# Turning the softmax weights of three batches by a transposing DMA instead of TensorE, in an attention and Fourier-filter kernel with a searched instruction order

## The chip, the core and the metric

The kernel runs on one core of a Trainium2 chip. A core has five engines that run side by side and wait for each other through semaphores: TensorE (PE: matrix products and transposes, with PEld for its weight loads), VectorE (DVE), ScalarE (ACT), GpSimd (POOL) and SyncE (SP, which here only issues DMAs). The metric is the time of one execution on the device, in microseconds; the median of three runs of the kernel before is 189.91 us (189.7 to 190.37).

## What is computed

For each of 8 batches and 8 heads, 32 packed queries attend to 576 keys; then 576 queries attend to the 32 packed results, used both as keys and values. The result, 576 x 512 in a batch, is projected to three parts, the second part is convolved with a filter along the sequence (by Fourier transforms), the three parts are multiplied, and the product is projected once more.

```python
def sm_attn(qq, kk, vv):
    s = scale * np.matmul(qq, kk.transpose(0, 1, 3, 2))
    a = np.exp(s - np.max(s, axis=-1, keepdims=True))
    return np.matmul(a / (np.sum(a, axis=-1, keepdims=True) + 1e-09), vv)
p_packed = sm_attn(p, k, v)              # 32 rows a head
x = sm_attn(q, p_packed, p_packed)       # 576 rows a head; heads are then joined to 512 columns
x1, x2, x3 = split(x @ w_proj)
x2_conv = np.fft.irfft(np.fft.rfft(x2, n=S, axis=1) * H, n=S, axis=1)
return (x1 * x2_conv * x3) @ w_out       # 8 x 576 x 512, float32
```

## The kernel before

The 32 packed rows of each head make it cheap to keep the second attention in factors: the softmax weights `a2` of one batch are 576 rows (sequence) x 256 columns (head, packed row), and the packed values times `w_proj` are `qm`, 256 x 1536. The three parts `x1`, `x2`, `x3` are products of the two. Each batch passes four stages, and four batches are in work at a time, one in each stage:

- `front`: first attention, scores of the second attention, exponentials, and the normalised weights `a2` (GpSimd writes them for all batches but the first);
- `turn`: `qm`; the Fourier transform of the weights (`fp`, `fpt`, then `fa`); and the **turned weights** `a2t`, with the 256 columns on partitions, in two halves `t`;
- `middle`: the spectrum times the filter (`f`, then `gm`), and the gate `w = x1 * x3` from products of `qm` with `a2t`;
- `back`: the inverse transform (`x2`) times the gate gives `y`, and the output projection `o` is stored.

The weights lie in one buffer of 128 partitions x 1152 columns: four row tiles of 256 columns each, and a fifth, joined tile of 128 columns for the last 64 rows. The turning before is done by TensorE into PSUM and copied by VectorE:

```python
# turn(b)
for t in range(2):
    tp = pst(f"a2tp_b{b}", [P, S], FP16)
    nc.tensor.transpose(tp[:, ds(COL0[4] - 64 * t, P)], a2c, ident)
    for i in range(4):
        to = tp[:, ds(COL0[i], P)] if i != 2 else ...     # [cut] tile 2 goes into two pieces of 64
        nc.tensor.transpose(to, a2n[:, i, ts(t, P)], ident)
    nc.vector.tensor_copy(out=a2t[:, t, :], in_=tp[:])
```

```python
# middle(b): four gates of 512 columns (one a part m), and one of 64 columns for all parts
x1, x3 = psm(...), psm(...)
for x, c0 in ((x1, 0), (x3, 2 * DM)):
    for m in ms:
        for t in range(2):
            nc.tensor.matmul(x[:, m - ms[0], :], qm[:, t, ds(c0 + m * P, P)], a2t[:, t, cols],
                             start=(t == 0), stop=(t == 1))
nc.scalar.copy(out=x1s[:], in_=x1[:])
nc.vector.tensor_tensor(out=w[...], in0=x1s[:], in1=x3[:], op=ALU.mult)
```

The queries of batches 4 to 7 and the keys of batches 6 and 7 are turned by transposing DMAs already (`TURNED`, `KEYS`), issued from SyncE. The last product of the kernel is the fifth row tile of batch 7. Its two column halves go through two PSUM tiles; ScalarE copies one and VectorE the other, and two DMAs of 64 rows x 512 columns store it, one from SyncE and one from ScalarE:

```python
for u in range(2):
    rows = out[b - 1 + u, 0:512, :].rearrange("(p i) c -> p i c", i=4)
    (nc.sync, second)[u].dma_start(rows[64:128, 3, :], os_[64 * u:64 * u + 64, :])
```

No operation is issued in the order in which this code stands. A recorder takes all operations down and issues them in an order of its own: a string of priorities (`PRIORITY`, one number for each operation), which a search found, is played against a model of the engines' times inside the kernel file. All engines' instructions therefore carry the same source line (L538), and rows of the profile are told apart by the names of tiles. At the start TensorE is kept busy by products that nothing uses (`spin`).

Of the kernel before, what the change touches and what calls it, by code (L numbers as in the profile page):

```python
# [14 lines left out]
FP16 = mybir.dt.float16  # L15
# [4 lines left out]
P = 128  # L20
# [23 lines left out]
def _constants(S):  # L44
# [42 lines left out]
    'c-oy-2|QHm`#)ziBV@}q$-b}ILqe1#S<_+(QCblyS-Q3q6)7nx*OIa&WG5L#Qp%bw`;vWM;+D?&kC{0$!@d8{?{|OiG0r*f`<(aLzR&l0g<vs='  # L87
    '-skz=M^>B>C98^O79=;F+~z2#*^_&Aw(_gw@3h6d`$6M;p%eO@bfY=Fi=#RWN-2G@iNBm%a|9kab)~&68y;M>&-z&J>u@98+tu6WNM5tTp1|z#'
    'qN=p|rB#7u465h(xW9?n6X6(xO9%Y5o!Y~Vd5uTyvI9)Kk{_km+>Y2kq&E`(wW?P9sFRkdd!Sr^NE}AYes9%X?nBnbHmZ_nD-Bnas&><q?Gdd@'
    'agRzO9Fs4eI)1LutKQ+6yGz~G@Al~}em{~bQltED8=tkdw>WMUq+8?k^4OId=CA0)CUW!yJMK1h$A^2>XrHn<=si!HtR58dY7^%lTfApvBP(j}'  # L90
    'XK1H#MvGZi2Wh<=RN*mR3Ti#4ZRBGnWvrmze8J~}flqdhj1?a@tLLPO-KJTUX{YU%gA*f#YdP}n^tMYCwvDSg>leK~BH%1@WQaM_M%9T=PUB?X'
    'ZNCl=5AztGcz<EZH~dD8o>?L)TmO8V=kd$l)U2K-cHqeS4zwuGiM{S%C~vW(*VE9)(9JM5h3cXi-|Ml8<t)%=&!Q&>r6rE$u|9?z?(KcA{=p~2'
    'WY1y1W@QGqS;LH%|A&_L@z9f27oDSnnVpXDT~s#H_ElnbK5OM;d_j%<x*Ux?!yaX<l%j~Xw~?UKG`lX1oVp>~sxnV%xfQ#R=d%9MR9i00`{vFF'
    'lpvS1%pvy|ZPIRs9tYU%E!=j4u@Y;8jj!GJu-D}JPFv1=FRlrbmRaA218rDgjc`9%u+l2~1WPLK$-}SA1w4=V3tmv86_XyGw_n=6IwG#lHl)uc'
    'HO;MFtrvo808<2A_z&q%Vqe}^Rw@r>URiBD9C5CdcUW~-{554`eJ_*#DD!Wjz0m?~P{|CtUsvI-r(*UdahGo&4e2_;&BnBNStAatUoCUDoaE3?'
    'YDO<-)ckh*8vlDx;+)sPKm2ACs>QxzSOSHXxii&(FNRY!$)I%sdM*oVj`m265bg3{%S!G!@6~T$F&A6!`nvC3t1{1=k{?s2q7jFq>c0K9tzSFp'
    'a;AMHx?Kzfop-tJwDdLdm*6?6z$L^jZ+1d=hnb)0aeXzc-Whj)b_ruMN!`<W7p#wK$;nr0sVi}SUh!|EP7K;^MPHRQ)DFTLS=_xDqNv6(+cMsp'
    '08}ybEYk|{*$Bxn6ktS8@6%c3?3&`brYGg#>=k-2Le6%}t<<Q74-RVKAJ00)+WILgSEhSq+J}0FCwWAL-8*&5x@!L0W5(mUhwlV4J`r)2ZVa!%'
    ';(A1~2Esn+XDKJkq8TDJm_&*muvzU~)Irr4<Vx2HCXJSX#h+suRHkbF<P3X1UO!Z(Q{G*Rdb(6m)1KF{qNNq3e@5T$_ioeQbK4GYI$3Z6Ug>1#'
    '%#Ij$Po1h;3ZyxLxhf$b#QyA7<;`7RO}&e6mseJQoG3D#%zeh8a(*wLoVv=2x-h?~+X+2-Md|HIEYb?9iu^pg#94LpC2V%esbZJ4nYH$a@`~)_'  # L100
    '4tw*`o9zf+#Oe5nkHbr%g+_73+vsc?<TMSO1NVI5f5OTr|4~)>y<Z2%F?7EDDyPIN!(YsaQOceM=&`d(Sdm|hBJ7fX<<QP;OMLFtv7lq_cyCEi'
    'R-)ohVGHe7{g*}TI&{bH4@Eodr=fRYm6(s8$eL_lO2;|&UhH-0I-VEsywW2}HT=}djDkl9t*th{i2QGPld6Ly^qjRu(_@b^uEl6BajQ!4H<as%'
    'E{MjqT1>cz38x64#<VTpK7E~#_eXl!8&!<YL}TKZY<CJawAH6f%$dPp(SkQ)I;ME;fJ<Q1)pT6Z$mJEObA8`3%jZvo_}_oqnp*tjTxMCv$|Hdg'
    'lS0o^F6k~ISTie~u3(v+d`zmn<z;gXEkECmRgZnCrb+5-eewO<yBEE6_3yHq^P5sfvOab7eEwP)*I6=FTer~mSMj}6QF#H)@f$x*`FeC1F4b=x'
    '>M(ED3jd?kp3YuNyx&qx!tTKS)fP_I=IwKD_KRAp+IZQR7#JzA#JMd_?o4NmMTJUfObbYHpJ1z2qZguuB6}HSIRy(w>hr#>pa#Y)ZC>Y>%eU+f'
    '9Gr>#)HiU;Oih+;cu(;sZ@X)W?;@U`PCs4{Q~j=6RBH5?13w!Zzp`OGZ+Z9Ng$mD7W1L5@Wq`YvSFnX+LF=qM!>=7Y+a|Bw;+O9hKJb#QVrS%R'
    'acUde*N7KIv1Xp{s`wv#iOlR3K!>PADHaU<tm|D^$R0o|&^|WGIGh}meKl8;WzeZP>R{O2=Ald7I@aY41%ti8QggLU35?ssN8)^~3!Z?`ZadaX'
    'X`d4PT3%c`jnm3%sX+5=UKJ`k>t?Le!oM(ab5U40kA>aCh5ulua5c_7@wQuRwEMl={+Ay(2Ho-Uwfo~j?7cUJcWtjbI%_&#*74cD$NzAc+wFU1'
    ';l{yN4NymD`_-77r$4W*4%s}4?B5rK^LKb(9crN+_;V^>^U7Jrm^v=ruM4w`heV=^)7k@sVghpG-&)KZ{B$rbIk^G8LPM{|I|7)y(eB?X<6h-#'
    'ZrZs;*Tz%c!qX#8mgVf{=(wYA<i9)Azm6BIj=p<K_<2HR8msu7i?lL&30~*gbn;VC=iGnH+VDM9YoM<<G$@&~t4#fAcy_?U8@K&e>1Usf>QDaE'  # L110
    'Qi*is!<cS6irsb0H_SZ#v4H7Jt;Oc>olEDxT{E<f-aWEoyvg<uss}wh^j4eRO-tE0=sOGjwYxV1!Xg4M#iupp&9_%_wQm~ChZ2~al48=oEj{d*'
    '4y?`U&dI<fgyKHr)r8>^s*?um3!BsDlY+X_@4mV9BsJ~X%gBz37hzB7jGbB-yzb&UKBmW|NQ5}szdzX>)RWy*FW6V}>GgtT;_8)WuQDzs%XDmi'
    ')&05j`ZDv(Hfc^x-ATjCZi1{^VsTe;Ubg*ta)^aXceCawn^Ov#Xq#Ko3!I+cxffgA^}^ymsAI)hCYYA`mZy7P756q^goa}y+yZZS1EK;l82Gh<'
    'Z|$$CG`WMS1{3#cidB7YWO^TE9uE`XY1`)%rg3q<$`zM@ikO@OU2b{V+;aW%!;4GIM+=L&gsYT3WBb_4?p(~ayr)s<d9@^PuF3%YxZK}GJmV<N'
    'w~X%afV8BQtomSurLC@oDLwZgldp6sbQQgqJxv*lR5f>vt{T;adFNg@!`wH_q}af`{V!%7GzV>{#jlh58M||72U*$C$|ZFbzgG&|8k<&{D$8+`'
    '#nr_FjkW#tDY&A+?)1j&k@5Vh{+jZ^sZTZ4RrO=N<;NA3V|KjoJ#l1e_c<JcH*S(;{`u+Pcpv|$Or3z+$rtVC-X@mD#CR|D50B5I{KhALeV=X9'
    '>-+I#q^Zwt{#Pf9NrCAOqs-VJu5X^Y#pHWrVB32ZAXkT^QpRjX2p8`ck@7g~No-1OaLaJZCDvQt#p$s-w(2c$-i2ce%S$@y25iJPVU=WVHGdvs'
    'US2urNShJeUz?Xwno)~;RGRtnQFLN;Q)vKu2@}RxoxU+xzbMip!#Gwa-0G!i#+S;>&n4xr^P@OYq_N=|yw(9(jePO<6K1g-Y+M2#@}sqqf~O+j'
    '(|=uFO*#+3Qo98?=<>><C&lP~bVq1_JY8RNJ}vg$E3Mh~F;+E+_qzH02fl_qyb8IF#uYg;35F}Dw_n@e*;Q)idWQYS=yxV<UM0&9T(QXm%3@m-'
    'RciH5UvhQ*smqxhHTw2!RaFK19aix;&bce|FC|1d->Y$5WC)-a=Qb?hPnGA8i9|hYzu)_4aiS|jpy{gbN@`k>U{PiXlcv%@nYelGSpLVy2bd>W'  # L120
    'Wps8hXM`l)EctdPKmWJ&yrizAPD|?3telW+AA4W@F1Cd0X=dJA1!<p4lz!w<y|OZ^waIb2gzN*Ay>$tVEy_avNBj0PWU~D_%k`%Fyt4-1F`L{x'
    '$*yswxm79Fy6TddvW2l1_m_pci>7cKDxxL&N*G2a9$a`>Uq7h)w7+Oc<Q+RN-*oS?n5@DCYAcO0!{$byZspqyN|+mtp(`0a79Y|ZUd@hLnr^RW'
    '{7h5&p3RqOv8`nZJ^AAcCZ7(2+3e8SIC`jWVi|w|7=;4xfA|68e;|kgQ7909BfQZ7AYmQ`2^ap3pMXiCYd69(2oPTZ@-8rG5Y}Osynx&Y3#7-j'
    'ZDB+Rkpch|@<7^{C;<P<LDWvQKUo7vRF3y}ZICn&rI1MwZv^q8d`c1}O09hZ0@UuoWC!pXA;bt$$kwJHV!#L!_>aN0T|k(q4u(;rcu|%K14T3+'
    'c?H*Y0jUP?Uk$Ql1pVZIfK*`xVNw|2HCxu)C71&unI`N3!5}fR01{ysL=nsf)*QsU4Xt?&0pu?L5J@{Z&SZE%q=ofKgEp8=3JCr`MAQL6L^b3c'
    'Ng@a|0W>A~00u*i2co9{8G^L5)WG`vF9*>A3<g6>9cx00kX%v)n{cPaP$sBAO~L~KZZO#wa*{ww(C}75gt2a47$ye_fJv%B(gX2Jh+L7B?8C$`'
    '!o;KkWLd;m5F{akIzbx{^&bF7KoL1ZFcJ_DVG*L?Bvg^1MqO7(nkiI42Irbrz#0HyB-_9$wEiNO2u#TY3A}{=5Jas4zXDNMib7=|Ou!rxC87XC'
    '9W$6jYg7Y8PAy^kO=t?00e>T^|4e2`Fp>J(geLj`!W4c*Ds%0H293sR#M}LwXgfeAB_y7R9W=z9NYq4@p;^<g(F_nqNErmEfI$Hsl0Z^`A+l1U'
    'G`NBC$=pMIt%E;`T0M%2RjHzge?n2U7QBTtG*n#&2L9y$i3I@?3yly>8l;X8d=kI|A+FHS5HymrNp2M|Qp1Q5C>lao@S6h&nQp|vTBlj-%Orq-'
    '8yNwn>WUld4hakdfdG+?DS-cn+NCH4VCY{CczvTI%mHM6#{WR1%J3RdD2U<&saQd3Y$II;M8T8@!w9PJCleH*<Vd;^>&XdPg9bp^4llnEyC{JA'  # L130
    'Sb%Ud@mgaE=%4BiqMS_#{STsAfv6HkPBe&^4Ezs+N-K=8_y5ZdAo%z4{6}FzoJl={dKQ0}AiDx>@R|~NsvNKLcVp+K*Z@+zq4d9X)~(|~gp4S-'
    'qLdZ5?#w`uCc~LfSQJPC8yOR(YK;K!Psd1L-Ek2hn+a{~Jft0=zZpYTgFul~8k7~n;f1h5=IFl}LUl~0q>{p=z`EuIuS*UU@c@*Q*?NxrKThot'
    '$p'
)

# [69 lines left out]
class Tick:  # L205
    n = -1
# [338 lines left out]
def kernel(  # L545
# [11 lines left out]
    nc = Recorder(tc)  # L557
    B, H, S, D = q.shape
# [593 lines left out]
```

## Time and profile before

| what | value |
|---|---|
| time, median of 3 | 189.91 us |
| span of the profiled execution | 187.6 us |
| TensorE | 175.1 us busy, 93% of the span, 2363 products |
| VectorE | 145.3 us busy, 77% |
| GpSimd | 138.0 us busy, 74% |
| ScalarE | 122.2 us busy, 65% |
| DMA | 31.96 MB in 49002 packets |

The page counts an engine as busy from the start of an instruction to its modelled end. TensorE's products are pipelined: the next starts long before the one ahead of it has ended, so the duration of one in the table of groups is its latency, and what a product costs in a dense stream is the distance from its start to the next start. A run of n equal products in the timeline lasts one latency and n - 1 such distances. In the chain of waits, followed back from the last instruction, each step is put down to what released it.

### The profile page before, as it was taken

How to read it: one execution, taken by the hardware profiler on the slowest of the kernel's cores; microseconds unless marked ns; L12 is line 12 of the kernel's file. 1: busy time of each engine (PE TensorE's matmuls, PEld its weight loads, DVE VectorE, ACT ScalarE, POOL GpSimd, SP SyncE). 2: the span in 40 equal slices, each digit the busy share in tenths (PEclk: the TensorE clock that was granted, in tenths of full speed). 3: DMA queues.
4: the chain of work that ended last, by engine and by line, in shares of the span. 5: the costliest groups of instructions: out<-in, count | busy, mean ns of one | idle time of the engine just before them, and what ended most of it. 6: DMA issues, size and time to landing. Idle time of an engine off the chain costs nothing.

```text
span 187.6 us, 5689 instructions
## 1 busy us (share of the span) xinstructions
PE 175.1 (93%) x2363; PEld 112.5 (60%) x2363; DVE 145.3 (77%) x274; ACT 122.2 (65%) x261; POOL 138.0 (74%) x111
## 2 busy tenths in 40 slices
PE   0999879999999999999999999999999999999990
PEld 0456546666756766865577557657655566555770
DVE  7368797967569789977789978977688898796560
ACT  2457757758989988667965496469659934434240
POOL 7533447795966899989949997799189979979300
PEclk9999999999999999999999999999999999999997
DMA  5999999999999999999999999958601500332374
GB/s 145 297 200 196 204 204 201 259 203 188 200 227 275 177 202 192 148 131 188 263 197 225 158 156 200 179 133 272 166 2 59 169 3 0 121 103 59 121 256 131
DMA packets 49002, 31.96 MB, mean 170 GB/s; under 512 B 21008, under 2 KB 43920, under 8 KB 48976
## 3 DMA queue, kind: packets, MB, share of 16 engines
q0 software_dynamic: 29456, 17.11, 64.4%
q1 hardware_dynamic: 18944, 13.70, 31.7%
q10 hardware_dynamic: 576, 0.79, 1.6%
q8 instruction: 18, 0.29, 0.7%
q14 instruction: 8, 0.07, 0.1%
HBM read 35.39 MB, written 9.44 MB: 239 GB/s over the span
## 4 chain that ended last, share of the span: by engine, by line
PE 82%; DVE 7%; POOL 4%; ACT 3%; issue 1%; POOLq 0%; DVEq 0%
PE x_b L538 29%; PE o_b L538 17%; PE f_b L538 9%; PE fp_b L538 5%; PE s_b L538 4%; PE hp L538 4%; PE pv_b L538 3%; PE kTp_b L538 3%; PE qp_b L538 2%; PE a2tp_b L538 2%; DVE zs L538 2%; PE spin L538 1%; DVE tt L538 1%; POOL tt L538 1%; POOL a2n L538 1%; PE qTp_b L538 1%
## 5 line engine op out<-in xcount | busy, mean ns | idle before, releaser
L538 PE MATMUL x_b<-a2t,qm 128*128 128x64 f16 (+1 forms) x256 | 46.1, 286 | 0.8 <-ACT qm L538 0.7
L538 DVE TENSOR_TENSOR tt<-f_b,h 128x1024 f32<-128x1024 f32 x32 | 38.6, 1219 | 5.6 <-PE f_b L538 5.2
L538 POOL TENSOR_TENSOR gm<-tt,tt 128x512 f16<-128x512 f32 (+1 forms) x30 | 39.6, 1346 | 0.9 <-DVE tt L538 0.3
L538 POOL TENSOR_TENSOR tt<-tt,tt 128x1024 f32<-128x1024 f32 x14 | 33.2, 2378 | 8.5 <-DVE tt L538 8.4
L538 PE MATMUL o_b<-wout,y 128*128 128x512 f16 (+1 forms) x144 | 38.2, 356 | 0.0
L538 PE MATMUL x_b<-ac,gm 128*128 128x64 f16 (+3 forms) x300 | 36.6, 249 | 0.0
L538 ACT COPY x1s<-x_b 128x512 f32<-128x512 f32 (+1 forms) x40 | 21.8, 545 | 16.4 <-PE x_b L538 10.8
L538 DVE TENSOR_TENSOR w<-x1s,x_b 128x512 f32<-128x512 f32 (+1 forms) x40 | 24.7, 628 | 7.1 <-ACT x1s L538 4.5
L538 PEld LDWEIGHTS <-gm 128*128 128x128 f16 x300 | 23.1, 98 | 10.0 <-issue 1.0
L538 ACT ACTIVATE os<-o_b 128x512 f32<-128x512 f32 (+1 forms) x36 | 20.0, 572 | 11.2 <-PE o_b L538 10.8
L538 ACT CAST qm<-qp_b 128x512 f16<-128x512 f32 x48 | 25.4, 605 | 2.6 <-PE qp_b L538 2.5
L538 ACT ACTIVATE e<-s_b 96x384 f16<-96x384 f32 (+1 forms) x48 | 23.5, 524 | 4.2 <-PE s_b L538 3.7
L538 PE MATMUL f_b<-qm,fa 128*128 128x512 f16 x80 | 25.3, 379 | 0.3 <-POOL fa L538 0.3
L538 DVE SCALAR_TENSOR_TENSOR y<-w,x_b 128x512 f16<-128x512 f32 x32 | 21.2, 682 | 5.3 <-PE x_b L538 5.0
L538 PEld LDWEIGHTS <-qm 128*128 128x128 f16 x256 | 17.9, 98 | 11.3 <-ACT qm L538 1.2
L538 PEld LDWEIGHTS <-a2n 128*128 128x128 f16 x240 | 16.6, 98 | 9.1 <-DVE a2n L538 1.6
L538 POOL TENSOR_TENSOR fa<-ez 128x512 f16<-128x512 f32 x15 | 19.0, 1275 | 2.7 <-ACT ez L538 2.6
L538 POOL TENSOR_TENSOR a2n<-e,zr 128x1152 f16<-128x1152 f16 x7 | 14.9, 2130 | 4.5 <-DVE zr L538 4.4
L538 PEld LDWEIGHTS <-y 128*128 128x128 f16 x144 | 13.0, 98 | 7.4 <-issue 0.8
L538 ACT COPY ez<-fp_b 128x512 f32<-128x512 f32 x16 | 9.3, 591 | 5.7 <-PE fp_b L538 4.6
L538 DVE TENSOR_REDUCE zs<-e 128x36 f32<-128x1152 f16 (+2 forms) x10 | 11.1, 1107 | 0.9 <-ACT e L538 0.8
L538 POOL DMA_DIRECT2D kn<-in_k_dram x8 | 6.5, 815 | 6.8 <-PE s_b L538 2.4
(82 smaller groups left out, 288.5 us busy)
## 6 DMA issues: line engine op xcount, KB each, us to landing
out_dram<-os SPq DMA_DIRECT2D x24, 256.0 KB, 2.4
kn<-in_k_dram POOLq DMA_DIRECT2D x8, 576.0 KB, 14.9
vn<-in_v_dram POOLq DMA_DIRECT2D x8, 576.0 KB, 11.1
qn<-in_q_dram POOLq DMA_DIRECT2D x8, 512.0 KB, 14.2
out_dram<-os SPq DMA_DIRECT2D x15, 128.0 KB, 3.2
wp<-in_moe_w_proj_dram POOLq DMA_DIRECT2D x3, 512.0 KB, 15.9
w<-in_moe_filter_fft_dram SPq DMA_DIRECT2D x2, 512.0 KB, 6.2
out_dram<-os SPq DMA_DIRECT2D x15, 64.0 KB, 2.1
```

Of the source, the lines that this page charges most:

```text
L538: ins = op.call(*op.args, **op.kw).ins
```

## The change

It has four parts.

- For batches 5, 6 and 7 (`FLIP`) the ten TensorE transposes and two VectorE copies of a batch go away. One transposing DMA from SyncE turns the whole buffer `a2`, 128 x 1152, into nine blocks of 128 x 128.
- The DMA leaves the columns in the order of the blocks, not in the order that the gate wants. So the products of the gate take their right operand in pieces for these batches: 512 columns become pieces of 256 (two blocks apart from each other), 64, 64 and 128 columns. For each piece the two halves `t` follow each other. The gate of the last 64 columns stays one product a half.
- The fifth row tile of batch 7 is stored by four DMAs of 64 rows x 256 columns instead of two of 64 x 512: two from each queue.
- The model's cost of the packets of a store is set from a rate of 22.7 to 18 bytes a ns, and the string of priorities is new, so that instructions on all engines stand in a new order.

The point of the first part is to take work off TensorE and VectorE and two PSUM tiles a batch; the last stores are cut so that one column half may leave before the other is ready.

```diff
+        s["a2t"] = sb([P, 9 * P], FP16, tag="a2t", name=f"a2t_b{b}")
+        if b in FLIP:
+            nc.sync.dma_start_transpose(s["a2t"].rearrange("p (x r) -> p x r", r=P), s["a2"][:])
 ...
-        for t in range(2):
+        for t in range(0 if b in FLIP else 2):
             tp = pst(f"a2tp_b{b}", [P, S], FP16)
 ...
+        def turned(t, cols):
+            if b not in FLIP:
+                return [(slice(0, cols.stop - cols.start), a2t[:, t, cols])]
+            if cols.start:
+                return [(slice(0, 64), a2b[:, 4 + t, 64:128])]
+            return [(slice(0, 256), a2b[:, 2 + t:7 + t:4, :]), (slice(256, 320), a2b[:, 8, ts(t, 64)]),
+                    (slice(320, 384), a2b[:, 4 + t, 0:64]), (slice(384, 512), a2b[:, t, :])]
 ...
-                    for t in range(2):
-                        nc.tensor.matmul(x[:, m - ms[0], :], qm[:, t, ds(c0 + m * P, P)], a2t[:, t, cols],
-                                         start=(t == 0), stop=(t == 1))
+                    for pieces in zip(turned(0, cols), turned(1, cols)):
+                        for t, (c, right) in enumerate(pieces):
+                            nc.tensor.matmul(x[:, m - ms[0], c], qm[:, t, ds(c0 + m * P, P)], right,
+                                             start=(t == 0), stop=(t == 1))
 ...
-                    (nc.sync, second)[u].dma_start(rows[64:128, 3, :], os_[64 * u:64 * u + 64, :])
+                    for c in range(split):
+                        c = ts(c, DM // split)
+                        (nc.sync, second)[u].dma_start(rows[64:128, 3, c], os_[64 * u:64 * u + 64, c])
 ...
         if self.reads and self.engine != "POOL" and piece > 1000:
-            self.piece_ns = piece / 22.7
+            self.piece_ns = piece / 18
 ...                                            # and a new string PRIORITY
```

## The prediction

> **What bounds the kernel now.** I read the page's busy times and its chain of waits first, then TensorE by stretches of time and the waits of TensorE alone.
>
> ```profile
> PE 175.1 (93%) x2363; PEld 112.5 (60%) x2363; DVE 145.3 (77%) x274; ACT 122.2 (65%) x261; POOL 138.0 (74%) x111
> PE 82%; DVE 7%; POOL 4%; ACT 3%; issue 1%; POOLq 0%; DVEq 0%
> 30.00:90.00 60.00, 59.50 (x983) 40.34 (x981) 48.10 (x93) 48.32 (x105) 51.03 (x41) 1.00 1.38 200
> 90.00:130.00 40.00, 40.00 (x572) 25.93 (x571) 34.84 (x60) 27.79 (x65) 34.43 (x25) 1.00 1.18 195
> PE spin L538 <- DVE ppk L538: 4.8, 1, 4.8
> PE x_b L538 <- ACT qm L538: 0.7, 1, 0.7
> PE a2tp_b L538 <- DVE a2n L538: 0.7, 2, 0.4
> ```
>
> The third and fourth lines are stretches of the trace: length, then TensorE's busy time (59.50 of 60 us, 40.00 of 40 us), weight loads, VectorE, ScalarE, GpSimd, granted clock 1.00. TensorE is the bound from about 30 us to the last product. Its waits (the last three lines: us in total, times, longest) are a start of 4.8 us and then less than 1 us each, all in the first 30 us or so. So work that TensorE is spared is nearly all gain, and work that VectorE or GpSimd is spared gains nothing by itself. After TensorE comes a tail:
>
> ```profile
> 182.64 0.38 ACT L538 ACTIVATE os<-o_b 128x256 f32<-128x256 f32 x1 [0.38 <-PE o_b L538]
> 183.05 0.53 ACTq L538 DMA_DIRECT2D out_dram<-os  x1
> out_dram<-os ACTq DMA_DIRECT2D x1, 128.0 KB, 3.3
> ```
>
> The last copy starts at 182.64 us, the last DMA is issued at 183.05, it takes 3.3 us to land (third line: size, then us from issue to landing), so 186.4; the remaining 1.2 us to 187.6 are the program's end.
>
> **What one product costs.** In the timeline of TensorE a run of n products lasts one latency and n - 1 distances from start to start:
>
> ```profile
> 147.39 0.51 PE L538 MATMUL x_b<-ac,gm 128*128 128x64 f16 x12
> 151.47 0.72 PE L538 MATMUL x_b<-ac,gm 128*128 128x288 f16 x5
> 153.97 0.33 PE L538 MATMUL a2tp_b<-wc,a2n 128*128 128x128 f16 x3
> 154.60 0.49 PE L538 MATMUL fp_b<-wc,a2n 128*128 128x256 f16 x3
> 148.39 1.27 PE L538 MATMUL x_b<-a2t,qm 128*128 128x512 f16 x12
> ```
>
> The first: latency 0.193 us (the groups' mean for 64 columns), so (0.51 - 0.193) / 11 = 29 ns for 64 columns, each with its own weights. The third: latency 0.220, (0.33 - 0.220) / 2 = 55 to 56 ns for 128 columns, which is what a transpose costs. The fourth: (0.49 - 0.272) / 2 = 109 ns for 256. The last row mixes 512 and 64; 512 alone, start to start, is 216 ns (153.10 to 153.97 us in the same timeline holds four). The weight loads, 98 ns each in the groups, hide behind products at every one of these sizes.
>
> **What the Trainium skill says.** Three places bear on this.
> - "TensorE: Matmul & The Clock Gate", section "Back-to-back issue gap", gives N/2.4 + 2.5 ns for an isolated warm product, so 29, 56, 109 and 216 ns: the trace agrees. The same section gives some 81 ns as sustained for a stream of weight loads and products of 128 columns; this trace shows 56 with weight loads in between, and I take 56.
> - "VectorE: DVE Perf Modes", section "The three transpose paths", puts a 128x128 transpose at 390 ns on TensorE and 1309 ns by DMA. In this trace TensorE pays 56 ns of its stream for one, and a whole transposing DMA of 128 x 576 lands after 2.6 us; both are far cheaper when many follow each other.
> - "DMA: Bandwidth & Descriptors", section "Issuing engines are not separate DMA queues": DMAs of all engines share the same 16 and interleave. The trace agrees: turning the keys took 8.0 to 12.7 us around 97 to 100 us while inputs were loading, and 2.6 once they were in.
>
> **The change, part by part.**
>
> (1) Transposes leave TensorE: 3 batches x 10 x 56 ns = **-1.68 us**.
>
> (2) The gate is cut in pieces. One product of 512 columns (216 ns) becomes four of 256, 64, 64 and 128: 109 + 29 + 29 + 56 = 223 ns, 7 ns more. There are 2 parts (x1, x3) x 4 gates x 2 halves x 3 batches = 48 of them: 144 more products, **+0.34 us**. Weights now change at every product of 64 columns, but so they do in the 29 ns run above. Net with (1): **-1.34 us**, 2363 products become 2477.
>
> (3) VectorE loses 6 copies of 0.454 us (the group of a2t copies), 2.7 us, and six PSUM tiles are not needed. Neither ends a wait of TensorE in that part of the run: I count nothing for it.
>
> (4) The transposing DMA. 128 x 1152 is 1152 packets of 256 bytes. The last of the key transposes is the nearest measure (their three numbers are min, median and max):
>
> ```profile
> L538 SPq DMA_TRANSPOSE kT<-kn x4: 1215/1268/1353, 117.4 to 122.3; - x4
> DMA to landing us min/median/max: 2.6/2.8/4.6
> ```
>
> These hold SyncE for 1.25 us and land after 2.6 us with 576 packets; the packets themselves flow within some 0.7 us. Twice as many: an estimate of 2.6 + 0.7 = 3.3 us, up to 4, on a quiet queue. Is that hidden? I added up TensorE's start-to-start times in the instruction order of both built programs; the sum stands 10.8 us behind the clock of the trace from 30 us on in the kernel before. For batch 5 the gate comes some 18 us after the first `fp` product that reads the weights, for batch 6 some 9 us: hidden, even at the 8 to 12 us of a loaded queue for batch 5. For **batch 7** it is tight. Its first gate product stands at 142.4 + 10.8 = 153.2 us. GpSimd finishes the weights after two `fa` of batch 6 and four `gm` of batch 5: last `fp` product of batch 6 at 127.7 + 10.8 = 138.5, its copy to 139.4, two `fa` (1.25 us each) to 142.0, four `gm` (1.25) to 147.0, weights (2.12) to 149.2. Plus 3.3 to 4: landing at 152.5 to 153.2. I expect a stall between 0 and 1 us and count **+0.2**.
>
> (5) The tail. In the new order the ScalarE half of the last tile comes first on TensorE and the VectorE half last. VectorE's copy (0.42) ends as late as ScalarE's did, about 0.45 us after the last product's start plus its latency. Then only 64 KB a column half are left to leave instead of 256 KB, but ScalarE's and SyncE's queues have three and four short issues to make, 0.4 to 0.5 us each, so the last leaves about 0.5 us later than before. Stores of 64 KB land after 1.9 to 2.1 us instead of 3.2 to 3.3. Sum 0.5 - 1.2 to +0.1: I count **-0.3**.
>
> (6) The new order everywhere. The first 20 us hold the same 8 + 17 `spin` products and the same filter products, in another sequence; the small `p` load now goes ahead of the keys, and the transpose of `p` stands earlier in TensorE's order. The waits there are worth some 5 us in all, and a new order may win or lose a part of them: 0, with an uncertainty of 1 us.
>
> Sum: 189.9 - 1.34 + 0.2 - 0.3 = 188.5; I say **188.6 us**, 0.7% less.
>
> **Rivals.** (a) *The DMA is the new wait.* The gate of batch 7 waits for its turned weights, or the weights' DMA of batch 5, first in SyncE's queue, holds back the key and query transposes of batch 7 behind it. For it: SyncE issues in order; in the kernel before one query transpose held the queue for 7.88 us. Against: in the new order the query transpose of batch 7 stands behind the keys', and the first product of those keys at 117.9 + 10.8 = 128.7 us; before, the last of them was issued at 122.3 and landed 2.6 later, so there are some 4 us to spare, of which the weights' DMA takes 2. It would give 189.5 to 191.5 us. (b) *The pieces cost more than their columns*: a right operand of two blocks apart, or weight loads that no longer hide. At the weight load's 98 ns for each of the 4 x 48 pieces it would be 192 x 98 = 18.8 us instead of 10.7, so 197 us; the runs of 64 columns at 29 ns speak plainly against it. (c) *VectorE or GpSimd bound a stage that looks TensorE-bound*, so that sparing VectorE 2.7 us and PSUM tiles lets TensorE close gaps: at most the waits after 30 us, about 1 us, so 187.5. (d) *The new order itself*, tuned on a model whose stores are slower, is worse or better at the start: plus or minus 1 us.
>
> **Range and chances.** The certain part is -1.34 us. (a) and (d) can eat it all; (c), (d) and the tail can at best double it. I take 187.3 to 190.3 us for 8 in 10. Two per cent would be 186.1 or 193.7 us: faster by more than that would need gaps that TensorE doesn't have, slower would need (b) or a long stall of (a). Chances 0.04, 0.92, 0.04.
>
> **What would show it.** Right, if the profile after has 2477 products, the gaps of TensorE after 30 us are still under 1 us each, the last product starts about 1.3 us earlier than 182.3 us, the transposing DMAs of `a2t` for batches 6 and 7 land 3 to 4 us after issue, and 64-column gate products stand 29 ns apart. Step 4 is wrong if the gate's products wait for the DMA of `a2t`, or if SyncE is held. Step 5 is wrong if the last landing is not 2 to 3.5 us after the last copy. Step 6 is wrong if the first product after the scores of batch 0 starts at another time by more than half a us. The prediction as a whole fails if TensorE's stream no longer sets the end.

## The result, and the profile after

The changed kernel takes **189.45 us** (median of 6 runs) where the kernel before takes 190.39 in runs beside it: a ratio of **0.9953, 95% interval 0.9932 to 0.9974**, so 0.9 us less, with 0.5 to 1.3 us in the interval. A second set of 22 runs gave 0.9959 (0.9944 to 0.9974). The forecast, 188.6 us against a base of 189.91, was a ratio of 0.9931: the direction is right, the time lies inside the range, but the gain is smaller than forecast. Two remarks on numbers. The base of 189.91 us came from three runs; beside every later kernel the kernel before had medians of 190.2 to 190.4, so from here on only ratios are compared, and a ratio is turned into us with 190.3. And one profile is one execution, while executions of one kernel differ by 1 us and more, so a difference of a few tenths between two profiles proves nothing by itself. The two profiled executions here took 189.39 us (before) and 189.49 us (after): the first lies 0.9 us below its kernel's median of 190.3, the second at its median, so the gain can't be read from this pair.

The lines of the page that answer to those of before (busy time of each engine; the chain of waits by engine):

```profile
PE 174.5 (93%) x2477; PEld 117.0 (62%) x2477; DVE 143.3 (76%) x268; ACT 123.5 (66%) x261; POOL 137.8 (73%) x111
...
PE 66%; DMA 24%; POOL 3%; ACT 2%; issue 2%; DVE 0%; POOLq 0%
```

2477 products, as forecast, and 6 copies fewer on VectorE. But the chain that ended last now has 24% of DMA in it, where none showed before. That is less than it sounds: the chain follows, at each step, whatever came last, however short the wait for it. TensorE by stretches of time (length, then busy time of TensorE, weight loads, VectorE, ScalarE, GpSimd), and TensorE's waits (us in total, times, longest):

```profile
30.00:90.00 60.00, 59.12 (x1000) 40.28 (x998) 48.50 (x94) 48.69 (x108) 49.73 (x40) 1.00 1.42 203
90.00:130.00 40.00, 39.99 (x554) 25.40 (x539) 34.48 (x60) 27.50 (x61) 34.69 (x26) 1.00 1.29 183
...
```

```profile
PE spin L538 <- DVE ppk L538: 4.6, 1, 4.6
PE a2tp_b L538 <- DVE a2n L538: 1.2, 1, 1.2
PE x_b L538 <- DMA ac<-c_ac: 0.5, 1, 0.5
```

TensorE is idle for 0.88 us between 30 and 90 us, against 0.50 before. The third wait is new: at 38 us the inverse transform of batch 0 waits for its constants `ac`, a plain load. The chain (start, length, what) reaches loads by another wait, TensorE's 0.3 us for `fa` at 53.6 us:

```profile
2.92 12.24 DMA vn<-in_v_dram
15.45 14.48 DMA kn<-in_k_dram
...
32.15 17.70 DMA vn<-in_v_dram
51.43 0.78 POOL vn L538
52.22 1.30 POOL fa L538
```

Read downwards: a load of values, then one of keys, then one of values that lands at 49.9 us; GpSimd issues the next loads and computes `fa` in one queue, so its work stands behind the loads. Up to some 52 us this execution had a chain of input loads, 12 to 18 us each, that ended 0.3 us behind TensorE's own work; TensorE was still busy 59.12 of the 60 us.

The turned weights themselves, in the view of the tile `a2t` (the issue's hold of SyncE in ns, min/median/max; time to landing in us; who waited):

```profile
L538 SPq DMA_TRANSPOSE a2t<-a2n x3: 1470/1943/2282, 114.9 to 150.4; - x3
...
  PEld L538: 0.2, 1
...
DMA to landing us min/median/max: 3.7/3.9/8.6
```

Batches 6 and 7 land after 3.7 and 3.9 us, batch 5 after 8.6; 0.2 us of waiting. The tail, in the timeline, and then from the table of DMAs (size, us to landing):

```profile
180.94 4.06 SPq L538 DMA_DIRECT2D out_dram<-os  x5
...
181.94 0.89 DVE L538 TENSOR_SCALAR os<-o_b 128x256 f32<-128x256 f32 x2 [0.74 <-ACT os L538]
...
182.45 1.64 ACTq L538 DMA_DIRECT2D out_dram<-os  x3
```

```profile
out_dram<-os ACTq DMA_DIRECT2D x3, 64.0 KB, 2.1
```

VectorE's last copy ends at 182.83, 0.2 us earlier than the last copy before. But of the five issues in SyncE's line four follow each other from 182.43 to 185.0; the last of them starts at 184.40 and lands at 186.3, where before the last landing was at 186.4. So nothing of the copy's 0.2 us is left at the end.

### The profile page after: what moved, and what is told of

Same layout as the page of the kernel before. It is cut to its first block, busy times and chain, and to the rows that moved or that the text cites. A ratio compares the mean times of both kernels' runs of the same rounds, so it can differ in the third digit from the quotient of the medians.

```text
span 187.7 us, 5930 instructions
## 1 busy us (share of the span) xinstructions
PE 174.5 (93%) x2477; PEld 117.0 (62%) x2477; DVE 143.3 (76%) x268; ACT 123.5 (66%) x261; POOL 137.8 (73%) x111
## 4 chain that ended last, share of the span: by engine, by line
PE 66%; DMA 24%; POOL 3%; ACT 2%; issue 2%; DVE 0%; POOLq 0%
PE x_b L538 26%; DMA vn<-in_v_dram 16%; PE o_b L538 15%; PE f_b L538 8%; DMA kn<-in_k_dram 8%; PE fp_b L538 4%; PE s_b L538 3%; PE qp_b L538 3%; PE pv_b L538 2%; PE kTp_b L538 1%; PE fpt_b L538 1%; ACT qm L538 1%; PE a2tp_b L538 1%; POOL qn L538 1%; POOL fa L538 1%
## 5 line engine op out<-in xcount | busy, mean ns | idle before, releaser
L538 PE MATMUL x_b<-a2t,qm 128*128 128x64 f16 (+3 forms) x400 | 45.7, 243 | 0.0
L538 DVE TENSOR_TENSOR tt<-f_b,h 128x1024 f32<-128x1024 f32 x32 | 38.5, 1219 | 4.4 <-PE f_b L538 3.2
L538 PE MATMUL x_b<-ac,gm 128*128 128x64 f16 (+3 forms) x300 | 38.9, 249 | 0.5 <-DMA ac<-c_ac 0.5
L538 PE MATMUL o_b<-wout,y 128*128 128x512 f16 (+1 forms) x144 | 35.4, 356 | 0.0
L538 PEld LDWEIGHTS <-qm 128*128 128x128 f16 x400 | 25.1, 98 | 9.4 <-issue 1.1
L538 ACT CAST qm<-qp_b 128x512 f16<-128x512 f32 x48 | 26.1, 608 | 3.1 <-PE qp_b L538 3.1
L538 DVE TENSOR_TENSOR w<-x1s,x_b 128x512 f32<-128x512 f32 (+1 forms) x40 | 24.5, 628 | 2.9 <-PE x_b L538 1.9
L538 PEld LDWEIGHTS <-gm 128*128 128x128 f16 x300 | 22.2, 98 | 7.0 <-POOL gm L538 1.4
L538 PE MATMUL f_b<-qm,fa 128*128 128x512 f16 x80 | 24.7, 380 | 0.3 <-POOL fa L538 0.3
L538 PEld LDWEIGHTS <-a2n 128*128 128x128 f16 x210 | 14.0, 98 | 6.9 <-DVE a2n L538 1.7
L538 POOL DMA_DIRECT2D qn<-in_q_dram x8 | 7.2, 901 | 6.4 <-PE s_b L538 2.4
```

What stands on the lines that cost most here:

```text
L538: ins = op.call(*op.args, **op.kw).ins
```

## The experiments

A word on how the variants are made. The searched priorities give one order of all instructions; in the variants that order is frozen as a list, and single entries are put in, taken out or moved. "Old order" is the list of the kernel before, "new order" that of the changed kernel. Two comparisons of traces help where whole times are too coarse. TensorE's progress can be set against the sum of its start-to-start times (the sum used in the forecast): where the trace runs away from that sum, TensorE loses time. And two kernels in the same order can be compared product by product: how much later or earlier does the same product start?

### Each part of the change alone

**e2, the transposes gone.** Old order; for batches 5 to 7 the transposes and their copies are left out, and the gates read the weights of an older batch that the buffer still held.

```diff
-        for t in range(2):
+        for t in range(0 if b in (5, 6, 7) else 2):
             tp = pst(f"a2tp_b{b}", [P, S], FP16)
```

> The kernel before in its own order, with the 30 transposes and 6 copies of batches 5 to 7 left out and nothing in their place: the gate of those batches reads what an older batch left in the buffer, so the output isn't the reference's. Theory A: TensorE saves 30 x 56 ns, 1.7 us less, ratio 0.991. If sparing VectorE 2.7 us and six PSUM tiles counts as well: over 2 us less, ratio 0.989 or below.

Measured: 0.9927 (0.9907 to 0.9947), so 1.4 us less, 1.0 to 1.8. The 1.68 us of step 1 are in the interval. Its trace shows something that was not on the list, in ScalarE's waits:

```profile
ACT os L544 <- DMA out_dram<-os: 0.7, 2, 0.4
```

ScalarE, copying output tiles near 131 us, found no free buffer: a store of an earlier tile had not landed. In the trace of the kernel before ScalarE has no such wait. TensorE had come to this place earlier, and 0.4 us of it went back in the group of `qp` products that needs ScalarE. Product by product, TensorE is 0.25 us behind the kernel before at 110 us and 0.48 us ahead of it at the last product: of the 1.68 us taken out there, 0.7 arrive.

**e3, the pieces alone.** Old order, transposes kept; the gates of 512 columns cut at 256, 320 and 384, as in the change.

```diff
-                    for t in range(2): matmul(x[:, m - ms[0], :], ..., a2t[:, t, cols])
+                    for lo, hi in zip(cut, cut[1:]):          # (0, 256, 320, 384, 512)
+                        for t in range(2): matmul(x[:, m - ms[0], lo:hi], ..., a2t[:, t, c + lo:c + hi])
```

> The kernel before in its own order, weights turned by TensorE as before, and only the gate products of batches 5 to 7 cut into pieces of 256, 64, 64 and 128 columns. Theory A: 48 x 7 ns, 0.34 us more, ratio 1.002. Rival B (pieces cost more than their columns): 0.8 us more or above, ratio 1.004 and up.

Measured: 0.9997 (0.9982 to 1.0012), -0.3 to +0.2 us. Step 2 had +0.34, so the pieces cost a little less than that; product by product, 0.06 us between 110 us and the last product. Rival (b), 7 us more, is out.

**e1, turning by DMA in the old order**, each DMA right behind the write of its weights in the list, the last tile stored as before.

> The kernel before with its own instruction order kept: only the three transposing DMAs (each set right behind the write of its weights), the gate in pieces, and the 30 transposes and 6 copies taken out; last stores as before. Theory A (the turning is worth its 1.34 us of TensorE, and the new order gave a part back): 1.3 us less than the kernel before, ratio 0.993, so faster than the changed kernel by about 0.4 us. Rival B (the turning itself is worth only the 0.9 us that the changed kernel shows; the order is neutral): ratio 0.995 or more. Rival C (the turning needs the new order, because SyncE or the DMA is held in the old one): no gain or slower.

Measured: 0.9962 (0.9941 to 0.9982), 0.3 to 1.1 us less, in 22 runs from 188.4 to 194.6 us, where the kernel before beside it went from 189.8 to 192.0. So the turning alone, without the new order, gains about what the whole change does, and scatters. The trace has ScalarE waiting 0.7 us for stores and the weight loads 0.6 us for keys, both near 130 us: rival (a) had named SyncE's queue. Product by product, it gains 0.9 us on the kernel before between 110 us and the last product, where steps 1 and 2 had 1.34.

**e4, the new order without turning.** `FLIP = ()`, the new order and its four last stores, the TensorE transposes put back in, 14 TensorE instructions ahead of the first gate that needs them.

> The changed kernel's order and last stores, but the weights of batches 5 to 7 turned by TensorE again, 14 TensorE instructions ahead of the first gate product, and the gate whole. Theory A (new order worse than the old by about 1 us): 1.0 to 1.5 us slower than the kernel before less the spread of the runs, ratio 1.003 to 1.008. Rival B (order neutral): equal to the kernel before, ratio 1.000.

Measured: 1.0033 (1.0020 to 1.0047), 0.6 us more than before. This run does not isolate the order: in its trace TensorE loses 1.1 us more than before between 30 us and the end, and 0.6 of that stands beside the transposes that I put back. So it shows no gain from the new order, and no more than that. The order is compared better between e5 and e7 below: both with the turning and two last stores, the one in the new order, the other in the old, 0.9933 and 0.9934.

**e6, four last stores in the old order.**

```diff
-    (nc.sync, second)[u].dma_start(rows[64:128, 3, :], os_[64 * u:64 * u + 64, :])
+    for c in range(split):
+        c = ts(c, DM // split)
+        (nc.sync, second)[u].dma_start(rows[64:128, 3, c], os_[64 * u:64 * u + 64, c])
```

> The kernel before in its own order, with only the last row tile stored in four column halves. Theory T: no change, ratio 0.999 to 1.001. Rival (the prediction's tail): 0.3 us less, ratio 0.9985.

Measured: 0.9998 (0.9988 to 1.0008), 0.2 us less at most. Step 5's -0.3 us is not there, in this order.

### The tail in the new order

**e5** is the changed kernel with the two stores of before instead of four; **e9** the changed kernel once more; **e10** is e5 with the last but one small store of SyncE moved ahead of its big one.

> The changed kernel with its own order, but the last row tile stored whole again, by two DMAs of 64 x 512 issued once both halves are copied. Theory T (the four short issues eat what smaller stores save): the same as the changed kernel within 0.2 us, ratio to the kernel before 0.994 to 0.997. Rival (the prediction's tail): 0.3 us slower than the changed kernel, 0.997.

> The changed kernel itself, beside the next one on the same chip. Ratio to the kernel before 0.995, as measured. Its difference to the next run is the price of the four last stores.

> The changed kernel's order with two whole last stores, and SyncE's store of 32 rows moved ahead of the last tile's store. Theory F (the four stores cost the changed kernel 0.3 to 0.4 us by their number of issues behind the last copy): ratio 0.992 to 0.9935, 0.4 us or more below the changed kernel. Rival (the difference between 0.9953 and 0.9933 was noise): 0.995.

Measured: e5 0.9933 (0.9912 to 0.9954) in 6 runs, e9 0.9959 (0.9944 to 0.9974) in 22, e10 0.9955 (0.9935 to 0.9976) in 20. After e5 I held the four stores to be the loss; e9 and e10, side by side, have equal medians, 189.5 and 189.6 us. Six runs were too few to rank kernels 0.2% apart. The traces say more. Take the time of a profiled execution less the start of its last product, so that nothing TensorE did before is in it:

| what | runs | from the last product's start to the end, us |
|---|---|---|
| old order, two stores | before, e3, e15 | 7.06, 7.18, 7.17 |
| old order, four stores | e6 | 7.18 |
| new order, four stores | changed, e9, e13 | 7.40, 7.33, 7.33 |
| new order, two stores | e5, e10, e12, e16 | 6.77, 6.74, 6.76, 6.74 |
| old order, two stores, no transposes on TensorE for batches 5 to 7 | e1, e7, e11; e2 | 6.43, 6.42, 6.41; 6.88 |

Against the kernel before, the changed kernel's tail is 0.2 to 0.3 us longer, where step 5 had it 0.3 shorter; and in the new order four stores make it 0.6 us longer than two. SyncE's last issues of e5, to set beside the changed kernel's above:

```profile
181.04 3.45 SPq L547 DMA_DIRECT2D out_dram<-os  x4
```

One issue fewer in the queue, and the last store starts 1.50 us after the last product's start instead of 2.31 and lands 0.25 us sooner against it (3.98 instead of 4.23); the other 0.4 us is the end of the program after the last landing, 1.37 us with four stores and 0.98 with two. (In e4, new order and four stores too, the figure is 6.67: there the first of these stores is issued 0.36 us earlier against the last product.) The fastest executions of e9 and e10, 188.88 and 188.34 us, are about as far apart as their tails; that the medians are not means that TensorE came to its last product later in more executions of e10 than of e9. Why, or whether by chance, is open.

The last row holds a surprise that no step had: without the transposes the tail of the old order is 0.2 to 0.7 us shorter, though in e1, e2 and e7 the last store is issued 0.72 us after the last product's start, as before. It lands 2.8 us later instead of 3.3. The cause is not known. So part of what e1, e2 and e7 gain lies behind the last product, and is luck as far as the forecast goes.

**e8, one store per column half** instead of two, for both batches at once; the two stores of 32 rows of batch 7's last rows are joined in the same way, [2 x 32 x 512].

```diff
-    for u in range(2): ... dma_start(rows[64:128, 3, c], os_[64 * u:64 * u + 64, c])
+    both = out[b - 1:b + 1, 0:512, :].rearrange("u (p i) c -> u p i c", i=4)
+    (nc.sync, second)[c.start > 0].dma_start(both[:, 64:128, 3, c], os_[:, c])   # [2 x 64 x 256]
```

> The changed kernel with its own order, and the last stores in fewer issues: each column half of the last tile in one DMA of 128 x 256 (the first from SyncE, the second from ScalarE), and the two stores of 32 rows ahead of it in one. If the number of short issues behind the last copy is what the tail costs, the last issue comes at about 182.9 us in the profile's time instead of 184.4 and the kernel is 0.5 to 1.0 us faster than the changed one, ratio 0.990 to 0.993. If the landing of a DMA is what counts, it is the same, 0.995.

Measured: 1.0367 (1.0345 to 1.0389), 7 us more. The end of the trace, by stretches (the last two numbers are the DMA engines' share and GB/s):

```profile
185.00:194.00 9.00, 0.00 (x0) 0.00 (x0) 0.00 (x0) 0.00 (x0) 0.00 (x0) 0.50 0.13 40
```

For 9 us nothing works but DMA, at a share of 0.13, which is 2 of 16 engines, and 40 GB/s. The Trainium skill, "DMA: Bandwidth & Descriptors", section "Why a DMA increments its semaphore by 16 and not by 1", says that the slowest dimensions of a transfer's two sides set over how many engines it is spread; on the output's side that dimension is 2 here. Share and page agree. The other stores have 32, 64 or 128 rows as their outermost dimension, and 64 KB of them land in 2.0 to 2.1 us (changed kernel).

### What takes the gain back in the old order

**e7** is e1 with batch 5's transposing DMA behind the key transposes of batch 7 in SyncE's queue. **e11** is e7 with an early start: the tile that the `spin` products read is zeroed first, and 27 of them are issued instead of 8, so that TensorE is busy from 1.2 us on.

> The run with the turning in the old order once more, with one thing moved: the transposing DMA of batch 5 stands behind the key and query transposes of batch 7 in SyncE's queue instead of ahead of the keys'. Theory D (that DMA, issued at 118.8 us for 3.0 us in the run before, held the keys of batch 7, whose products waited, and made the run's times spread): 189.0 us or less, ratio 0.993, and a narrower spread than 188.4 to 191.3. Rival E (the lost half of the gain lies elsewhere, at places where TensorE now comes earlier than its inputs): ratio 0.996 as before.

> The old order with the turning, the DMA of batch 5 behind the keys of batch 7, two whole stores; and TensorE started earlier: the clearing of the buffer that the idle products read is VectorE's first instruction, and 27 instead of 8 idle products stand ahead of the filter's. Theory G (the filter products at 427 ns instead of 216, from 3 to 11 of them in different executions, are a TensorE clock not yet up, and cost up to 1.3 us): 0.5 to 1.2 us less than without, ratio 0.987 to 0.991, and a narrower spread. Rival (the filter's inputs set the start): 0.9934 as without.

Measured: e7 0.9934 (0.9909 to 0.9959) in 6 runs; e11 **1.0032** (1.0008 to 1.0056), from 189.6 to 193.3 us. With the early start it is slower than the kernel before. e11's ScalarE, in its timeline (in brackets the idle time before, and its cause), then the waits of ScalarE and TensorE:

```profile
130.56 0.60 ACT L547 ACTIVATE os<-o_b 128x512 f32<-128x512 f32 x1 [1.21 <-DMA out_dram<-os]
...
132.42 1.57 ACT L547 ACTIVATE os<-o_b 128x512 f32<-128x512 f32 x3 [0.89 <-DMA out_dram<-os]
```

```profile
PE qp_b L547 <- ACT os L547: 0.9, 1, 0.9
```

The wait of e2 again, three times as long: 2.1 us of ScalarE, and TensorE's `qp` products behind it. **e15** is the same early start in the kernel before, with no weights turned.

> The kernel before with the early start alone: TensorE's warming products begin some 3 us earlier and there are 27 instead of 8 of them; no weights are turned. If the early start brings time (the first filter products then run at full clock): ratio 0.996 or lower, and the changed kernel's run with the early start (0.992) owes half of its gain to it. If an early start brings nothing because the inputs land when they land: ratio 1.000. If a start that is earlier makes the later stages collide with stores and loads (what the run with the old order and the early start, 1.003, might be): ratio above 1.002, with waits for stores near 130 us.

Measured: **1.0058** (1.0031 to 1.0086). So it is not the turning. SyncE's queue shows why; first the kernel before, then e15 (start, hold, what), then ScalarE's wait in e15:

```profile
104.32 13.00 SPq L538 DMA_TRANSPOSE qT<-qn  x2
117.42 6.14 SPq L538 DMA_TRANSPOSE kT<-kn  x4
123.61 10.26 SPq L538 DMA_DIRECT2D out_dram<-os  x14
```

```profile
105.01 14.01 SPq L545 DMA_TRANSPOSE qT<-qn  x2
119.13 8.44 SPq L545 DMA_TRANSPOSE kT<-kn  x4
127.61 9.40 SPq L545 DMA_DIRECT2D out_dram<-os  x14
```

```profile
ACT os L545 <- DMA out_dram<-os: 2.2, 2, 1.6
```

From 104 us on SyncE issues six transposing DMAs, and behind them the stores of output tiles, the first of which were copied at 107 us. The transposes hold the queue long while input loads are in flight: 13 us for the first two, before. In the kernel before the last load of values landed at 118.3 us and the first of these stores left at 123.6; in e15 the load, issued 0.3 us later, landed at 122.8 and the store left at 127.6. There are five output buffers; when stores leave late, ScalarE waits for one, and TensorE waits for ScalarE. Product by product, e15's TensorE is 0.3 us behind the kernel before from 43 to 123 us and 2.2 us behind from 139 us on: the loss is made here. The DMA side thus runs close behind TensorE, and where TensorE comes earlier or, as in this execution, the loads later, the gain is taken back. Why the early start made the load land later is open.

**e14** moves five of those stores ahead of batch 5's transposing DMA in e11's list.

> The run with the old order, turned weights, batch 5's transposing DMA behind the keys of batch 7, and the early start (ratio 1.003, ScalarE 2.1 us waiting for output stores near 130 us), with one edit: five output stores stand ahead of that transposing DMA in SyncE's queue. Theory S (SyncE's queue is the dispute: stores that stand behind a transposing DMA leave later, output buffers come free later, ScalarE and then the qp products wait): ScalarE's wait for stores falls from 2.1 us to under 0.7, TensorE's wait for os is gone, the median falls by 0.9 us or more, to 190.0, ratio 0.998, and the runs spread less. Rival (the early start or the turned weights themselves make it slow, the waits for stores are only a symptom): the ratio stays near 1.003.

Its 22 executions went from 188.4 to 193.5 us, with a median of 191.6; its ratio of 0.9958, which like all ratios here leaves out executions over 1.5% above the kernel's fastest, rests on 9 of the 22, and I do not use it. The trace still had 1.7 us of that wait, and 0.6 us for the turned weights, which now came late. Inconclusive.

**e17 and e18** take away what makes ScalarE wait: six stores of batch 2, the ones in front of the queue there, are left out, so that part of the output is not written; e17 in e11, e18 in e15.

```diff
-            if n in (0, 1, 3):
+            if b == 2 and n != 4:
+                pass
+            elif n in (0, 1, 3):
```

> The run with the old order, turned weights, batch 5's transposing DMA behind the keys of batch 7, and the early start (191.0 us, ratio 1.003), with six output stores of batch 2 left out: part of the output is not written. They are the six that stand in SyncE's queue right behind the transposing DMAs near 127 us, and whose buffers ScalarE waited 2.1 us for. Theory S (the late stores hand back what TensorE was spared): ScalarE's wait for stores near 130 us is gone, so is TensorE's wait for os, and the median falls to 189.0 or less, ratio 0.993 or less, with runs closer together. Rival (the early start makes TensorE slower, or the turned weights do, whatever the stores do): the ratio stays above 1.000 and the runs stay as far apart.

> The kernel before with the early start (191.9 us, ratio 1.006, ScalarE waiting 2.2 us for stores), with the same six output stores of batch 2 left out. Theory S: the wait is gone, the median falls by 1.5 us or more, to 190.4 or less, ratio 1.000 or less. Rival (the early start costs by itself): the ratio stays near 1.006.

Measured: e17 **0.9892** (0.9863 to 0.9922), 188.30 us, against 191.01 with the stores; e18 0.9977 (0.9956 to 0.9999), 189.63 us, against 191.91. Both fall by more than 2 us, and ScalarE's waits for stores are gone from both traces. In e17's timeline the two copies that had waited now follow at once:

```profile
130.60 0.59 ACT L547 ACTIVATE os<-o_b 128x512 f32<-128x512 f32 x1
...
131.57 1.56 ACT L547 ACTIVATE os<-o_b 128x512 f32<-128x512 f32 x3
```

Leaving stores out also takes their bytes from the DMA engines, so what is shown is that those stores take the gain back, not that their place in the queue alone does. The profiled execution of e17 was the slowest of its six, 189.78 us, and it shows the next thing in that queue: `PE s_b` waits 1.6 us for the keys of batch 7. And e17 against e18 is the turning with this obstacle gone: 188.30 against 189.63, **1.33 us**, where steps 1 and 2 had 1.34. From the two ratios it is 1.6 us, give or take 0.7, so that the last digit agrees is luck; and 0.2 us of it stand behind the last product (6.59 us from its start to the end in e17, 6.77 in e18).

### What takes the gain back in the new order

Besides the tail, what scatters the new order is loads, not stores. ScalarE waits only 0.3 us for a store in the changed kernel. There one of the six stores of batch 2 leaves at 105.35 us, ahead of the transposes; the other five leave from 127.35 on, but after the copy at 128.92 the next copy that needs a buffer comes at 135.50, where in the kernel before there are three more between 129.78 and 130.74.

**e13** is the changed kernel with the load of `ac` ahead of the values and queries of batch 1 instead of behind them, in GpSimd's queue. **e12** is e10 with the early start, **e16** is e12 with `ac` ahead.

> The changed kernel with one load moved: the constants of the inverse transform (ac) are issued on GpSimd ahead of the values and queries of batch 1 instead of behind them. Theory A (the new order itself loses time because it puts the queries' load ahead of ac; TensorE's wait at 38 us in the changed kernel, 0.5 to 0.8 us, is a real loss): ac lands some 4 us earlier, the wait of x2 for ac is gone, and the median falls by about 0.5 us against the changed kernel: 189.0, ratio to before 0.993. Rival (the wait takes the place of another one that comes a few us later, fa or the projected weights): the wait for ac is gone, the other waits grow, and the ratio stays at 0.996.

> The same earlier start in the changed kernel's order with two whole stores. Theory G: ratio 0.987 to 0.991. With the run before it also tells whether the new order is worth anything once start and stores are equal: theory H (the order is neutral) expects the two within 0.3 us of each other.

> The best so far (new order, turned weights, two stores at the end, early start; ratio 0.992 in 6 runs) with the load of ac moved ahead as in the other run. Theory A: in this kernel the trace showed no wait for ac, so nothing or 0.3 us is won: 0.990 to 0.992. It also tells whether 0.992 stands again in another job. If that was the luck of few runs: 0.995.

Measured: e13 **1.0007** (0.9987 to 1.0026), e12 0.9920 (0.9894 to 0.9945) in 6 runs, e16 0.9947 (0.9920 to 0.9974). In e13 the wait for `ac` is gone, and this one has come:

```profile
PE qTp_b L547 <- DMA qn<-in_q_dram: 0.8, 1, 0.8
```

The rival was right: with loads pacing this part, moving one ahead makes another late. (The swap even costs 0.9 us against e9; its wait explains no more than a part of that, the rest is open.) e12 also answers the question that was put with it: against e11, the same start in the old order, it is 2.4 us faster (188.64 against 191.01), so the new order is worth something where the old one collides with its stores. Put side by side, the profiled executions of the new order with turned weights:

| run | that execution, us | last product starts | wait for `ac`, or for inputs of batch 1 | wait for turned weights of batch 7 | DMA in the chain |
|---|---|---|---|---|---|
| e12 | 188.69 | 181.93 | none | none | 4% |
| e5 | 188.96 | 182.19 | none | none | 3% |
| changed | 189.49 | 182.09 | 0.5 | 0.2 | 24% |
| e16 | 189.87 | 183.13 | 0.8 and 0.6 | none | 20% |
| e9 | 190.29 | 182.96 | 0.7 | 0.4 | 14% |
| e10 | 190.41 | 183.67 | 0.8 | 0.7 | 22% |
| e13 | 190.43 | 183.10 | 0.8 | none | 20% |

The chain of e12, and two waits of e10:

```profile
PE 85%; DMA 4%; ACT 3%; DVE 3%; POOL 1%; issue 1%; SPq 1%; DVEq 0%; ACTq 0%
```

```profile
PE x_b L547 <- DMA ac<-c_ac: 0.8, 1, 0.8
...
PEld L547 <- DMA a2t<-a2n: 0.7, 1, 0.7
```

e5 and e10 differ by one swap of stores at the very end, e9 and the changed kernel by nothing; yet their last products start 1.5 and 0.9 us apart, and the later ones have more waits for loads and turned weights. That is an observation over seven executions, not an experiment. Nor is it only a matter of when a load lands: `ac` landed at 38.47 us in the changed kernel and at 38.52 in e5, but in e5 TensorE came for it only at 38.7 instead of 37.9, having lost more at its start (below), so it had nothing to wait for. By the last product the two are 0.1 us apart; that e5 is 0.5 us shorter is its tail. What makes loads land later in some executions stays open.

e12 is the lowest median of whole kernels, 188.64 us, and beats the kernel before; against the changed kernel its interval overlaps, and e16, nearly the same kernel, gave 189.45. So no version here is shown to beat the changed kernel.

## Why the prediction was partly right and partly wrong

| step | forecast, us | measured |
|---|---|---|
| 1, 2: transposes out, pieces in | -1.34 | -1.33, e17 against e18, with luck; to the last product, waits included, -0.9 (e1) and -1.05 (e7) |
| 3: VectorE and PSUM count nothing | 0 | nothing seen |
| 4: wait for turned weights | +0.2, 0 to 1 | 0 to 0.7, by execution |
| 5: tail | -0.3 | +0.2 to +0.3 (traces); 0.0 in the old order (e6) |
| 6: the new order | 0, give or take 1 | 0.0, give or take 0.6 (e5 against e7); loads 0 to 0.8, by execution |
| sum | -1.3 | -0.9 (-0.5 to -1.3) |

The sum missed by 0.4 us, and step 5 alone by 0.5 to 0.6. Take the tail off, 7.1 to 7.2 us before and 7.3 to 7.4 after, and the medians put the last product some 0.9 to 1.2 us earlier: an estimate, which gives every execution the tail of the traces. Steps 1 to 4 and 6 had forecast 1.14. Of the 0.85 us between 188.6 and 189.45, the rest is the base of 189.91 us, from three runs, where six gave 190.39.

**Right.** The mechanism and the size of steps 1 to 2: 2477 products, and in the trace the median distance from the start of one gate product to the next is 29 ns for 64 columns, 56 for 128, 109 for 256. The transposing DMA's 3.7 and 3.9 us were forecast as 3.3 to 4. The wait for batch 7 was forecast as 0 to 1 us, and the place where SyncE would be in dispute was named in rival (a), though for the keys; in the old order it was mostly the stores that came late.

**Wrong, step 5, the step that failed.** Of its sum the term "the last leaves about 0.5 us later than before" was too small. The last store leaves at 184.40 us, 1.35 us later than before (183.05), because SyncE's four issues take 0.47 to 0.72 us each instead of "0.4 to 0.5" and start 0.56 to 0.77 us apart; against the last product, which starts 0.24 us earlier, it is 1.6 us later. The landing was about right: 1.9 us instead of 3.3, so 1.4 us saved, and the last landing is where it was. On top, the program's end after it, taken as 1.2 us, is 1.37. So the tail, forecast 0.3 us shorter, is 0.2 to 0.3 longer. (A column half is also 128 KB in two stores, not 64 KB.) The sign that I set for this step, a last landing 2 to 3.5 us after the last copy, was too wide to catch it: 3.5 us.

**Too simple, the reading under it all.** "So work that TensorE is spared is nearly all gain" fails in the old order, where e1 and e7 keep 0.9 to 1.05 of 1.34 us and, with the early start, e11 keeps nothing: late stores hold ScalarE, and ScalarE holds TensorE. In the new order it nearly holds, but for loads. Step 6, "The waits there are worth some 5 us in all, and a new order may win or lose a part of them: 0", put the order's risk into the first 20 us; but most loads take 12 to 18 us up to 52 us, and 7 to 15 us again between 92 and 124. In the kernel before `ac`, issued at 24.3 us, landed at 37.3, 0.8 us before its first use at 38.1; in the new order it is issued at 24.5, with the queries of batch 1 right ahead of it instead of three loads earlier, and lands at 38.5, while TensorE comes for it at 37.9. I had looked at which waits TensorE has, not at how much room the loads and stores leave it.

**The check that I set** also failed in its own terms: the last product was to start 1.3 us earlier, and does so by 0.24 (182.09 against 182.33). Most of that is chance: the profiled execution of the kernel before was 0.9 us shorter than its median, the other was not. One thing that varies so is the start, where the first filter products run at half speed for a different time in each execution (below).

## What to carry to other kernels

When one engine is busy 93% of the span, ask also how far behind it the next limit runs: look up when each load and store lands against when it is first needed, because time spared on the bound is worth no more than that distance. A queue that holds transposing DMAs and stores couples them: here a store behind a transpose was a late buffer, and a late buffer a wait of an engine that has nothing to do with either. Count the tail as a queue too: cutting a last store in two lands each half sooner, but the last half stands behind more issues (here +1.6 us of issue against -1.4 us of landing). And a gain below 1% is to be taken from ratios of many runs; a single profile tells where, not how much, unless parts of it are compared that come out equal from run to run, such as the stretch behind the last product.

## What the runs showed of the hardware

- **A store's outermost dimension of 2**: with three stores of 128 KB of that form the DMA engines worked on for some 10 us, at 40 GB/s (e8); stores of 128 KB with 64 rows outermost land in 2.3 us (median, changed kernel).
- **TensorE's start.** The same 14 filter products, in the kernel before and in e1 (start, time of the group):

```profile
6.50 4.05 PE L538 MATMUL hp<-gm,wc 128*128 128x512 f16 x14
```

```profile
7.01 5.28 PE L547 MATMUL hp<-gm,wc 128*128 128x512 f16 x14 [0.35 <-ACT gm L547]
```

  1.2 us apart for one list of instructions: in the first three products are 379 to 427 ns from the next, start to start, in the second ten; the others are 216, but for one between and, in the first, three waits of 0.08 to 0.19 us. With the early start (e11) it is the unused products that stand 214 ns apart and later 109, and all of the filter's stand 215 apart, but for four waits of 0.1 to 0.4 us among them: the half speed is gone from them, and 1.1 us of waits stand in its place. The Trainium skill, "TensorE: Matmul & The Clock Gate", section "Part 1: The HAM clock gate", says that the array starts at half its clock, comes up after some 4 us of activity, and that the number of slow products differs between executions of one kernel. The traces agree; the granted clock that the windows show for 6.5 to 14 us is 1.00 in both.
- **One transposing DMA holds its queue for anything from 1.2 to 9.7 us.** The four query transposes have one shape: in the kernel before they held SyncE for 5.28, 1.90, 7.88 and 5.02 us, in e3 one held it for 9.67 (at 103.7 us, while inputs were loading). `a2t` of batch 7, 1152 packets, held it for 1.35 us in e12, at 150 us, when no input was loading. No run separates what sets it.
